# Delta-rule attention fused with a gelu MLP: orders, loads, PSUM banks and constant matmuls dealt anew

## The chip, the core and the metric

The kernel runs on one core of a Trainium2 chip. The metric is the device time of one execution in microseconds (us), the median of several runs. Five engines work side by side, each through its own queue of instructions in order: TensorE (PE, matmuls; its weight loads are shown as PEld), VectorE (DVE), ScalarE (ACT), GpSimd (POOL) and SyncE (SP, which here only issues DMA transfers). They wait for one another on semaphores. Matmul results land in PSUM, which has 8 banks of 512 f32 per partition; everything else lies in SBUF.

## The reference

Attention by the delta rule over 4 batches, 8 heads, 768 steps and head dimension 48, whose output is the input of a two-layer MLP with 3072 tokens, 384 to 2048 to 384:

```python
k_n = k / (np.linalg.norm(k, axis=-1, keepdims=True) + 1e-06)
state = np.zeros((B, H, D, D))
for t in range(S):
    y[:, :, t] = einsum('bhd,bhde->bhe', q[:, :, t], state)
    v_old = einsum('bhde,bhd->bhe', state, k_n[:, :, t])
    state = state + beta[:, :, t] * einsum('bhd,bhe->bhde', k_n[:, :, t], v[:, :, t] - v_old)
x = y.transpose(0, 2, 1, 3).reshape(B * S, H * D)
out = gelu_tanh(x @ w_in) @ w_out
```

Only q, k, v, beta and the two weights come in, in float32; out goes out in float32. Matmuls are in bfloat16.

## The kernel before

The sequence is cut into 12 chunks of 64 steps. Within a chunk the recurrence is a triangular system, which is inverted; between chunks a state S (48 x 48 for each of 32 heads) is carried. For each chunk c:

- `load` (L480) brings k (tiles kf), q (qf, two chunks at a time) and v (vf) over SP's queue, the first k in part over ACT's. `load_w1`, `load_w1x` and `load_w2` (L515 to L539) bring the MLP's weights over POOL's queue, after the first q.
- `prep` (L592) squares k (sq, on ACT or POOL), sums it on DVE (ss, L603), takes the root on ACT (sr) and the reciprocal on DVE (rn); from chunk 4 on the root is a short series of DVE operations (`norms`). ACT's function table is loaded once for the root and once for gelu; the root's first use is a small warm-up operation at the start.
- `prep2` (L658) scales k (Kn, on POOL or DVE) and transposes it on PE (L680); `prepq` (L636) does the same for q (L648). Copies out of PSUM (KQT) go to DVE or ACT.
- `own` (L722) multiplies the chunk's keys by themselves in small blocks of 32; DVE transposes the result (Tt). `solve8` (L768) inverts the small blocks of chunk 0 on DVE; `solve` (L752) does it on POOL for chunk 1, and then for units of two chunks (unit 1 is chunks 2 and 3). The results are scaled (XW), transposed back on DVE (`back`, L802, tiles TB), and from the unit on, one part is shifted between partitions by a DMA on SP's queue.
- `gram` (L693) makes the products of keys and queries with keys: G by ACT, DT by DVE with a mask.
- `inverse` (L893) builds the whole inverse from the blocks: WB, DI, ET and TT, with PE matmuls between.
- `state` (L1020) makes R = K S - V, U = T R, the new S, and the chunk's output x.
- `mlp` (L1210) takes tiles of one chunk (tiles 0 to 3) or two (tiles 4 to 7): groups of matmuls with gelu on ACT behind each (L260, gT), then the second layer in halves of 8 matmuls, an eviction to osb and a store on ACT's queue.

The order of the work is not found on the chip. Every call of `op` (L102) records one operation with a number, its functions for the engines that can do it, its tiles read and written, and its PSUM allocations. `schedule` (L136) then reads the string `ORDER` (L18): a letter for the engine (p PE, v DVE, a ACT, g POOL, s SP) and the number of the operation. Each engine does its operations in the order in which they stand there; `emit` (L167) adds the waits that the tiles and banks ask for. A word such as w12.5 is not an operation of the program: it puts 12 constant matmuls (`spin`, L411, 128 x 512 on a tile of zeros) on PSUM bank 5, whose result nobody reads. The string `BANK` (L78) has one digit for each PSUM allocation, its first bank. The loop at the file's end (L1272 on) only records.

The lines where operations run are often helpers: L251 is `f_tt` (two tensors), L256 `f_cp` (copy), L260 `f_act` (activation), L267 `f_mms` (all matmuls but transposes and constants), L275 `f_dma`.

Numbers that the texts below speak of: 47 and 48 load k of chunk 0, 49 and 50 load beta; 2 is the warm-up root on ACT, 82 Square, 86 root and 88 reciprocal (rn0) of chunk 0; 89 and 90 make K0; 153 Tt0, 265 Tt1; 156 to 173 are chunk 0's solve; 180 DT0_0, 186 DI0_0, 192 ET0_1, 198 to 204 TT0; 217 the last matmuls for x of chunk 0; 266 to 299 chunk 1's solve on POOL with XW0 (299); 72 to 81 the weights' loads; 130, 390 and 393 make K of chunks 3, 4 and 5; 400 and 603 are the masks bM0 and bM1; 135 is a cast of q; 307 and 308 WB of chunk 1, 313 its ET1_0, 316 the matmul group that reads it; 398 and 399 `own` of chunks 2 and 3; 401 to 433 unit 1's solve; 437 its `back`, 462 WB of chunk 3, 466 the first matmul group that reads that; 435 and 436 the shift of TB; 342 the last matmuls for x of chunk 1; 224 to 238 the first-layer groups of MLP tile 0; 1274 the last matmul group.

Of the kernel before, what the change touches and what calls it, by code (L numbers as in the profile page):

```python
# [30 lines left out]
p228 v381 g410 v382 a313 s151 g411 v329 p136 g412 p137 s150 a229 g413 v383 p316 v138 p318 g414 s149 a317 v384 g415  # L31
p438 a227 v385 s223 p230 g416 v386 v139 a439 g417 s222 p232 a231 v387 g418 s148 v388 p320 a233 g419 v389 p459 v319
g390 s220 p234 a460 v440 s221 p322 a235 v321 p456 v461 p324 g420 a323 s396 a457 g393 p326 p441 s397 v327 a519 p236
v325 v458 p333 a442 g421 v520 p238 g422 a334 p391 g423 a253 v443 g424 p330 g425 a239 v331 p338 g426 p394 a252 v332
g427 v335 p339 v392 p340 g428 p341 a578 s259 p342 g429 p240 g430 v344 s260 g431 a343 g433 v579 a395 s258 p254 a237
g432 v580 p601 s345 v437 p602 s261 a444 v434 p241 s346 v462 s347 v604 p255 s348 a242 p349 s436 v256 g605 p351 a350
s435 v581 p644 v582 a352 p466 s531 v583 g521 p353 v584 a645 v585 s532 v445 p245 g522 a354 v646 a257 g606 v586 v587
g607 p355 g608 v464 a467 g609 p336 v588 v446 p448 g610 v337 p246 g611 a449 g612 v589 g613 v463 p523 g614 v590 a356
v591 p474 g615 v592 a247 p450 g690 a447 p357 v451 p359 v475 g593 p524 a360 p452 v525 a358 p468 g616 v453 a526 s599
p361 g596 v469 s600 p454 a362 p363 s527 v455 g617 v691 p476 s530 g618 p470 a477 g619 p480 s529 p594 g620 a364 p481  # L40
s528 g621 p478 a482 g622 p365 v479 s483 g623 a771 g624 s489 v471 p366 g625 s491 a595 v772 g626 s488 g627 g628 p533
a243 v773 s490 p662 v774 g629 p597 a244 v775 s492 g630 v776 p370 g631 a598 v777 s487 v778 g632 v779 g633 v780 s703
a367 g634 p371 v781 g636 v782 a692 s702 v783 v784 v785 g635 p794 v534 a372 a663 p795 v640 g786 a465 p493 v647 p495
v664 a494 g693 p472 v797 a496 p497 s792 g883 p499 v473 a498 s793 v637 p535 v648 s638 g796 p501 a536 v884 s699 p539
a502 p540 p641 g798 s486 v541 p694 a642 s639 p503 a500 v643 s700 g799 p695 a504 g800 p505 v696 g801 s548 p507 a506
s546 v697 p537 a665 s547 p651 g789 p659 v652 p509 s701 a508 s550 v538 a660 g802 p790 s549 g803 a374 p510 v661 g804
s698 a958 g805 v791 s551 g806 a249 v649 p837 g807 p669 v959 s484 p653 a248 g808 s485 p514 g809 a838 v654 g810 a668
g811 v670 a511 p515 g812 g813 v667 v839 g814 p552 g815 v960 a516 v961 p655 g816 v962 a553 p834 g817 v656 p677 a835
g818 p554 v963 g819 a650 v678 p556 g820 a555 g821 p657 v836 a557 g822 p558 v658 a886 g823 v666 g824 p679 g825 a559
p683 p671 g826 a680 g827 p560 g828 v672 p681 a561 p562 v682 g829 p673 a563 v830 p684 p704 v674 s832 a685 p564 v705  # L50
s545 p675 a565 s831 p852 v676 a369 p566 v964 s542 a853 v965 p710 v966 s544 p706 v967 a567 p568 v968 s543 v969 a707
v970 v841 a368 v854 p711 p855 v971 a712 p569 v860 v972 v859 g973 a856 v833 s719 p787 a373 v842 s720 p573 v857 a858
g885 s717 s721 p974 v840 a517 s722 p708 v788 p862 a570 g976 p574 s718 v863 a512 s688 v709 s687 g981 p864 a575 p977
s689 a576 v865 p887 s686 g1133 p888 v975 p723 v889 p844 a724 p725 v845 a861 p727 a843 v978 a726 p979 v890 a728 p980
p846 v982 p729 p731 v847 g983 a730 p1019 a732 p866 p1022 g984 v867 p848 g985 a1023 g986 p733 v849 g987 p735 g988 v1024
g989 p1131 a736 g990 g991 p1132 a734 g992 a1020 p737 g993 v1021 p739 g994 a738 g995 v1134 p870 a740 g996 p741 g997
p743 v871 a742 g998 g999 p850 a518 g1000 p868 a744 g1001 p745 v869 g1002 v851 p747 g1003 a746 g1004 p872 a748 p876
g1005 p749 a873 g1006 g1007 p751 a750 g1008 p874 g1009 a752 p877 g1010 v875 p753 a878 g1011 g1012 p1037 g1013 p891
a754 p755 v892 a577 g1135 a513 v1015 p897 a571 p893 s1016 g1014 p756 v894 a1038 s716 s715 g1136 v1018 g1137 p898 p1040
s714 g1138 a899 p759 g1139 s1017 v757 g1140 a1041 g1141 v1039 s713 p760 g1142 a572 v1043 s907 g1143 a1025 v1042 g1144  # L60
s906 p763 g1145 v1044 s904 v1026 g1146 a758 s908 g1147 v1045 v761 p1171 g1148 s905 p1029 a1172 p764 g1149 s909 a1028
g1150 v1173 s903 g1151 v1030 p767 g1152 a765 s881 g1153 v1027 s879 g1154 p1047 s882 g1155 p895 p1031 g1156 s902 p910
g1157 v1032 s880 g1158 p768 a911 g1159 v1048 g1160 g1161 p912 v896 g1162 g1163 p1174 g1164 a913 p1049 g1165 p1033 a769
v1050 a1175 p914 g1166 v1034 p916 a915 p1055 v1170 a917 p1051 p918 v1052 p920 v1177 a919 v1056 p1035 a921 p1053 a762
v1036 p922 v1176 p924 a923 p1057 a925 p926 v1058 a1046 p928 a927 v1195 p1061 a929 v1167 p1059 p1062 v1060 s1169 p930
a1063 s900 p932 v1054 a931 s901 p1068 p1074 a933 v1069 p1189 s1168 p934 a1190 p936 v1191 a935 p1070 a937 p938 v1071
a770 p940 a939 v1197 p1181 a941 v1179 p1075 p1192 v1196 a1076 p942 v1182 a766 s1080 p943 a1180 s1078 s1067 p946 v944
s1064 a945 s1065 p947 a1193 s1066 v1194 s1077 p950 v1178 a948 s1081 a949 s1079 p951 s1082 p1199 a952 p1072 p1183 a953
p954 v1184 v1200 p1083 p955 v1073 a1084 p1207 a956 p1213 v1208 p1185 p1085 v1186 p1087 p1201 a1088 p1187 a1086 p1089
v1188 a957 v1202 p1091 a1090 p1209 a1198 p1203 v1210 a1092 p1093 v1204 p1095 a1094 p1214 a1096 p1205 a1215 p1211 p1097  # L70
v1212 p1099 a1098 v1206 p1216 a1100 p1101 v1217 p1103 a1102 p1218 a1104 p1105 v1219 p1107 a1106 p1220 a1108 p1109
p1111 a1110 p1221 a1112 p1113 v1222 p1115 a1114 s1226 p1116 s1227 s1225 s1224 p1119 a1117 s1228 s1223 p1120 p1123
a1121 p1124 p1229 a1125 p1231 a1230 p1233 a1118 p1235 a1232 p1237 p1239 p1241 a1240 p1127 a1242 a1236 p1243 a1234
a1238 p1245 a1244 p1247 a1246 p1249 p1251 a1250 p1253 a1122 p1255 a1126 p1257 a1252 a1248 p1259 p1261 a1260 a1254
p1128 a1256 a1258 p1262 v1129 a1130 p1265 a1263 a1264 p1266 p1269 p1270 p1273 v1271 v1267 a1268 p1274 a1272 a1275
a1276
"""
BANK = ("6031340340660141100441256766766777042000503073120036766677667154142444144220200367676676760000276766"  # L78
        "7676754202240042244430024042067667677676767676767024104052244440000220220666767676767676767661042024"
        "2242042530200022767767667676767676764000444440000044210001203141021031450102")  # L80


class Op:
# [1256 lines left out]
```

## Time and profile before

| | us |
|---|---|
| runs | 249.78, 252.54, 251.93 |
| median of the runs | 251.93 |
| span of the profiled execution | 249.4 |
| PE busy in it | 232.0 (93%) |
| DVE, ACT, POOL busy | 161.4, 139.0, 118.6 |
| matmul instructions | 5637 recorded, 87 of them constant |
| DMA moved | 23.84 MB, 96 GB/s |

The profile is of one execution, on one core; its span lies 0.4 us under the lowest of the three runs. In the profile's groups each line gives the code line, engine, operation, the tile written and read, the shape, then busy time and the mean of one. A line of the chain gives start, length, engine, tile and code line. "Issue" is time in which an engine waited for nothing that the profile shows. The granted clock of PE is given as a share of full speed. Idle time of an engine that is not the bottleneck costs nothing by itself.

### The profile page before, as it was taken

The page shows a single profiled execution, that of the slowest core. Times are in us where ns is not written, and L with a number is a line of the kernel's source. Part 1 is how long each engine was busy: PE and PEld are TensorE (multiplying, and loading weights), DVE is VectorE, ACT ScalarE, POOL GpSimd, SP SyncE. Part 2 cuts the span into 40 slices and gives each one's busy share as a digit, 9 for nine tenths or more (in the row PEclk, how much of TensorE's full clock was granted, in tenths as well). Part 3 has the DMA queues.
Part 4 walks back from the last instruction along what each step waited for, and adds up shares of the span by engine and source line. Part 5 has one row for each costly group of instructions (what it writes and reads, how often), then busy time and mean ns, then how long its engine had stood idle before and what let it go on. Part 6 is the DMA issues. An engine that isn't in the chain of part 4 may idle for free.

```text
span 249.4 us, 12386 instructions
## 1 busy us (share of the span) xinstructions
PE 232.0 (93%) x5637; PEld 155.0 (62%) x5637; DVE 161.4 (65%) x316; ACT 139.0 (56%) x262; POOL 118.6 (48%) x249
## 2 busy tenths in 40 slices
PE   7577896998999799999899999999999999999995
PEld 4334473587778658868766655666656665555562
DVE  6699989886799399896969653767772465100001
ACT  2744578587686466838564357535682247426600
POOL 3685796688389858588045589883000000000000
PEclk9999999799999799999999999999999999999999
DMA  6999969996740825550244000623135210000112
GB/s 157 209 196 168 159 116 211 159 214 107 184 87 19 192 52 112 122 137 7 57 111 91 5 20 23 149 57 63 37 76 134 78 37 3 8 11 32 66 63 96
DMA packets 64789, 23.84 MB, mean 96 GB/s; under 512 B 53600, under 2 KB 63840, under 8 KB 64736
## 3 DMA queue, kind: packets, MB, share of 16 engines
q1 hardware_dynamic: 58656, 14.89, 30.8%
q0 software_dynamic: 1056, 3.15, 7.3%
q10 hardware_dynamic: 5024, 5.02, 6.3%
q8 instruction: 44, 0.72, 1.2%
q14 instruction: 9, 0.07, 0.1%
HBM read 20.64 MB, written 4.72 MB: 102 GB/s over the span
## 4 chain that ended last, share of the span: by engine, by line
PE 81%; DVE 10%; DMA 2%; issue 2%; ACT 2%; POOL 0%; ACTq 0%; POOLq 0%
PE ps L267 76%; DMA kf<-in_k_dram 2%; PE ps L648 2%; PE ps L680 2%; PE ps L414 1%; DVE ss L603 1%; DVE WB L931 1%; ACT WB L915 1%; DVE TB L806 1%; DVE KQT L256 1%; DVE ps L846 1%; DVE Yf L251 1%; DVE Tt L837 1%; DVE btz L251 0%; DVE ps L786 0%
## 5 line engine op out<-in xcount | busy, mean ns | idle before, releaser
L260 ACT ACTIVATE gT<-ps 128x512 bf16<-128x512 f32 x96 | 55.9, 597 | 38.4 <-PE ps L267 36.8
L267 PE MATMUL ps<-x,W 128*128 128x256 bf16 (+1 forms) x384 | 72.2, 329 | 0.0
L267 PE MATMUL ps<-W,gT 128*128 128x384 bf16 x384 | 67.0, 328 | 0.0
L267 PEld LDWEIGHTS ps<-W,gT 128*128 128x128 bf16 x384 | 36.4, 98 | 23.9 <-issue 0.5
L267 PEld LDWEIGHTS ps<-x,W 128*128 128x128 bf16 x384 | 39.1, 115 | 16.3 <-issue 0.3
L762 POOL TENSOR_TENSOR Yf<-Yf,tmp 128x28 f32<-128x28 f32 (+13 forms) x84 | 28.8, 342 | 6.4
L759 POOL TENSOR_TENSOR tmp<-Yf 128x28 f32<-128x28 f32 (+13 forms) x84 | 28.1, 335 | 6.1
L251 DVE TENSOR_TENSOR TT<-ps,DI 128x768 bf16<-128x768 f32 (+2 forms) x30 | 20.2, 684 | 13.8 <-PE ps L267 13.5
L414 PE MATMUL ps<-wz 128*128 128x512 bf16 x87 | 23.3, 416 | 1.4 <-DVE wz L409 1.4
L251 POOL TENSOR_TENSOR Kn<-kf,rn 128x768 bf16<-128x768 f32 (+1 forms) x11 | 16.0, 1452 | 17.1 <-DVE rn L629 10.1
L267 PE MATMUL ps<-KQT 48*32 48x32 bf16 (+1 forms) x1152 | 18.7, 195 | 5.8 <-issue 2.7
L260 ACT ACTIVATE osb<-ps 128x384 f32<-128x384 f32 x18 | 8.8, 490 | 26.3 <-PE ps L267 26.3
L256 DVE COPY osb<-ps 128x384 f32<-128x384 f32 x6 | 3.2, 552 | 29.8 <-PE ps L267 29.8
L260 ACT ACTIVATE G<-ps 128x512 bf16<-128x512 f32 x24 | 14.3, 597 | 11.4 <-PE ps L267 7.7
L267 PEld LDWEIGHTS ps<-KQT 48*32 48x32 bf16 (+1 forms) x1152 | 13.6, 95 | 10.9 <-issue 5.0
L719 DVE TENSOR_TENSOR DT<-ps,mD 128x512 bf16<-128x512 f32 x24 | 16.3, 680 | 4.1 <-ACT G L260 4.1
L267 PE MATMUL ps<-TT,ET 64*64 64x32 bf16 (+1 forms) x768 | 16.4, 176 | 0.0
L267 PEld LDWEIGHTS ps<-TT,ET 64*64 64x64 bf16 x768 | 14.8, 109 | 2.2 <-DVE R L251 0.6
L414 PEld LDWEIGHTS ps<-wz 128*128 128x128 bf16 x87 | 8.7, 105 | 11.5 <-issue 3.0
L251 DVE TENSOR_TENSOR S<-ps,S 128x768 bf16<-128x768 f32 x10 | 9.5, 953 | 9.0 <-PE ps L267 8.9
L260 ACT ACTIVATE x<-ps 128x1024 bf16<-128x1024 f32 (+2 forms) x10 | 9.2, 916 | 8.1 <-PE ps L267 7.9
L251 DVE TENSOR_TENSOR R<-ps,vf 128x768 bf16<-128x768 f32 x11 | 10.4, 949 | 3.8 <-PE ps L267 3.8
(122 smaller groups left out, 333.2 us busy)
## 6 DMA issues: line engine op xcount, KB each, us to landing
qf<-in_q_dram SPq DMA_DIRECT2D x24, 192.0 KB, 4.4
kf<-in_k_dram SPq DMA_DIRECT2D x23, 192.0 KB, 4.9
vf<-in_v_dram SPq DMA_DIRECT2D x40, 96.0 KB, 3.2
out_dram<-osb ACTq DMA_DIRECT2D x16, 192.0 KB, 2.0
W<-in_moe_w_out_dram POOLq DMA_DIRECT2D x4, 384.0 KB, 6.7
out_dram<-osb ACTq DMA_DIRECT2D x16, 96.0 KB, 2.8
W<-in_moe_w_in_dram POOLq DMA_DIRECT2D x4, 192.0 KB, 8.7
vf<-in_v_dram SPq DMA_DIRECT2D x4, 192.0 KB, 11.3
```

The lines of the kernel that those rows point to most:

```text
L251: return lambda e: e.tensor_tensor(out() if callable(out) else out, a() if callable(a) else a, b() if callable(b) else b, op)
L256: return lambda e: e.tensor_copy(out, a() if callable(a) else a)
L260: return lambda e: e.activation(out, a() if callable(a) else a, func)
L267: ins = t.matmul(out, lhsT, rhs, start=st, stop=sp_, skip_group_check=skip)
L414: ins = e.matmul(psum[:, b, :], wz[:, 0:128], wz[:, :], start=True, stop=True)
L603: op({"dve": 0.95 * w}, {"dve": lambda e, u=u: e.tensor_reduce(ss[j][:, u], sq[:, u, :], AX.X, ALU.add)}, reads=[f"sq{n}"], writes=[f"ss{j ...
L648: ins = e.transpose(o[:, a, j], Qn[:, n, a, j, :, :].rearrange("q h d -> q (h d)"), identB[:, :])
L680: ins = e.transpose(tb()[:, m, :], t[:, 2 * m:2 * m + 2, :].rearrange("p h d -> p (h d)"), identB[:, :])
L719: op(d_ps(512), {"dve": lambda e: e.tensor_tensor(dv, gview(1)(), md, ALU.mult)}, reads=[h] + MD, writes=[dn])
L759: sop(nb * s * w, lambda e, s=s, w=w, tv=tv: e.tensor_tensor(tv, yf[:, :, s:s + 1, 0:s].to_broadcast([128, nb, w, s]), Yv()[:, :, s + 1:16 ...
L762: sop(nb * s * w, lambda e, s=s, tv=tv: e.tensor_tensor(Yv()[:, :, s + 1:16, 0:s], Yv()[:, :, s + 1:16, 0:s], tv, ALU.add), [YN, TN], [YN])
L806: op({"dve": 0.58}, {"dve": lambda e: e.transpose(dst, src)}, reads=reads, writes=writes)
```

## The change

Only the two strings are other. The operations are the same 1276, with the same shapes, tiles and dependences. The orders of all five engines are new, and with them the places of the loads and of the constant matmuls: 85 in 11 groups (1, 10, 6, 13, 9, 3, 29, 3, 7, 2, 2) in place of 87 in 11 groups (6, 12, 1, 1, 8, 4, 29, 1, 3, 12, 10). Some fifty operations, most of them copies out of PSUM, change between DVE and ACT, a few between POOL and another engine. The digits of the banks are new. SP has 138 operations and POOL 238 in both; DVE has 306 for 307, ACT 269 for 268. Code lines behind the strings are one lower. The core of the diff:

```diff
-v34 a50 g11 s49 v5 v0 g21 v46 a48 s47 g22 v6 g16 v8 v35 v41 g18 s54 v1 v4 a2 g13 g14 s55 g12 g19 v15 v45 s53 a26 v43
-v33 v10 s56 v3 w6.7 p61 v36 v37 v9 v38 s51 v42 v7 v40 s52 a82 g84 v63 s60 a24 g20 v85 g17 a29 v39 v62 a30 a31 v83 a32
-a23 v67 a86 s59 v70 a87 v64 v88 s57 a97 g75 v89 v65 g81 s58 w12.5 p91 v66 a98 p99 g90 v44 v92 g77 w1.4 p93 a103 v68
-p100 v94 g72 g76 a101 s96 p152 v104 g74 v153 g73 a105 w1.7 p181 a106 a182 v107 v154 g108 v156 v155 g69 w8.3 p109 v157
-v158 v159 a110 v160 v183 g80 s141 a102 v161 w4.5 p264 v162 v163 v164 p178 v265 a179 v165 g266 v166 a117 v167 v168 v169
-v170 a25 a28 g267 a27 v171 g268 g269 v172 g270 g271 v173 g272 g273 v174 g274 g275 v175 g276 g277 v176 a185 g278 g279
-s95 a184 v177 w29.3 p191 g280 p301 g281 v192 g282 a187 p189 v186 g283 v190 g284 a188 w1.5 p195 g285 v118 p193 g286
-a196 g287 a194 p199 v71 g288 v180 p197 g289 a200 g78 a119 p203 v198 a120 g290 a205 p201 v121 g291 v204 v122 g79 a202
-p209 a302 p206 g292 g293 s147 v207 a210 g294 g295 a125 v208 s140 v211 g296 w3.5 p215 v303 p216 g297 p217 s146 p304
-v218 a219 p212 p123 v126 a305 g299 v298 a127 a128 v129 a133 v306 g130 v300 s115 v124 a213 s113 g400 w12.7 p131 v308
-a309 s116 p398 v132 a311 s114 g603 v214 p399 a250 s111 p314 v401 a310 s112 a315 v251 s144 g402 s142 a375 v307 s143
-g403 g404 w10.6 p312 v376 a135 s145 g405 p224 g406 s262 g407 p226 v377 a225 g408 v378 s263 v379 p328 a134 g409 v380
...
-g427 v335 p339 v392 p340 g428 p341 a578 s259 p342 g429 p240 g430 v344 s260 g431 a343 g433 v579 a395 s258 p254 a237
...
-s435 v581 p644 v582 a352 p466 s531 v583 g521 p353 v584 a645 v585 s532 v445 p245 g522 a354 v646 a257 g606 v586 v587
...
-a1276
-BANK = ("6031340340660141100441256766766777042000503073120036766677667154142444144220200367676676760000276766"
...
+v0 g21 s47 a48 v45 g18 w1.3 g16 v34 v44 a50 v33 g13 s49 v46 w10.0 g14 g19 s55 v35 v10 s51 s52 a82 g84 w6.0 v83 g11 v85
+g12 s56 g22 p61 g17 a86 s54 a87 g20 v88 s53 v3 v36 v9 v5 v37 v15 v89 w13.0 s58 v1 v62 a2 v38 a32 v90 a103 v7 s95 a30
+v104 a25 p91 p93 s59 v63 a105 a26 v92 a94 v64 v67 v4 g81 v65 a97 v70 p152 v6 s60 v42 g77 v66 a106 a23 p99 a98 v107
+v153 g108 a24 p100 v154 w9.5 a101 g76 v155 s140 a102 v156 s141 p181 a27 p109 a182 v157 v158 v159 p178 a31 v68 a110
+w3.1 v160 g69 v161 v162 v163 a179 v164 v39 p264 v165 v166 v183 w29.7 v167 v168 v169 g117 v170 s57 v171 v180 g79 v8 s96
+v265 g74 g72 v172 g266 v173 v174 g267 v43 v175 g75 w3.4 v176 a184 g268 g73 v177 a185 p189 g269 p304 v187 a28 a186 p191
+g270 v190 g271 w7.2 v71 g272 v118 a29 a192 g273 g274 g275 a125 p301 g276 p193 g400 p195 a302 v194 a205 v40 v196 p197
+g277 v41 g78 v303 p199 a198 a305 g278 p201 v126 g80 a200 a202 p203 a119 g279 v306 a120 a188 g280 v121 a204 g281 a127
+a250 p209 g282 p206 g283 v210 w2.3 a207 g284 a128 g285 a211 v208 v251 g286 p215 p216 g287 p217 g288 v129 v122 g289
+g290 a218 g291 v219 s146 p123 g292 g293 s147 g294 p212 g295 v124 g130 p228 v213 p224 a229 g296 p131 a133 g297 p226
+v132 s113 p398 s115 a225 g299 v298 p399 s114 p234 v401 s116 a375 s111 a308 v300 g402 s112 v376 a307 p314 g403 a227
...
+g411 p322 g412 w2.7 s150 a139 v388 v323 p438 v389 a321 g390 p459 p326 a460 p324 a327 v461 a439 p232 g413 s396 a519
+v440 g414 p456 s397 p236 a325 g415 v520 a457 g393 p391 a252 v458 p330 p338 a237 v331 p339 g416 p333 v392 a332 g417
+p394 a334 g418 p238 a253 v395 g419 p254 a335 g420 a239 s259 p340 g421 p341 a578 s143 p441 p342 g422 a233 s261 g423
...
+g431 v581 p336 g432 v582 v583 p255 v604 p245 a256 g433 v434 p241 v584 g605 v437 s532 v585 a444 v462 s436 v257 g522
+p466 s435 v445 p246 g606 s531 v337 a467 g607 g608 s220 g609 a242 g610 p448 v247 p644 p474 g611 a645 v586 g521 p351
...
+a1250 p1269 p1247 p1273 a1248 a1126 p1266 p1270 a1267 a1268 p1262 v1271 a1272 p1274 a1263 a1264 a1275 a1276
+BANK = ("7301720430530101010120307666677776016301010106204426767677767151240000442230220477766667764220066767"
...
```

Loads of k stand ahead of those of beta on SP and ACT (s47, s49; a48, a50). ACT's Square (a82) stands ahead of the warm-up root (a2). Tt1 (v265) stands inside chunk 0's solve (156 to 173), and the weights' loads g75, g73, g78 and g80, the mask g400 and K3 (g130) stand inside chunk 1's solve (g266 to g299). In unit 1's solve (g402 to g433) now stand g603 and g135 beside g390 and g393. Four first-layer groups of MLP tile 0 (p228, p224, p226, p234) stand ahead of or among `own` of chunks 2 and 3 and chunk 1's inverse (p312, p314, p316), where 12 and 10 constant matmuls stood.

More of the change, by code (lines that the diff above doesn't have):

```diff
@@ L39 @@
[L39 to L43, printed above, removed]
@@ new lines @@
+a362 s600 p454 a526 g617 p357 v455 g618 v595 s530 p476 g619 p480 v691 a477 s529 g620 p363 g596 a358 p481 a364 p478
+s347 p365 a482 v479 g621 g622 a771 s489 g623 p597 g624 s488 a249 p470 v772 g625 a465 s491 p370 a598 g626 v471 s702
+g627 v773 g628 v774 s490 v775 g693 p533 v776 p662 p794 s492 v534 a663 g629 p371 s703 g630 v777 v664 s487 g631 g632
+p366 g633 v372 g634 g635 v778 a373 v779 a692 p641 p795 g636 v637 a243 p472 a642 s639 p497 v780 a367 v781 s346 v782
+p501 v783 a498 v784 v785 a883 v473 p493 g786 v643 a502 v797 p535 a494 p539 a536 s793 p499 v640 g798 s638 p495 a500
@@ new lines @@
+v884 s345 p659 p540 a496 s348 g799 p694 v541 a660 g1133 p503 p507 v661 a504 s551 g800 g801 p695 v648 s792 a508 p505
+v647 a665 s699 v649 v696 p537 g802 s549 p651 g803 p509 a697 v667 s548 v652 g804 s484 g805 a506 v538 g806 p837 s546
+p834 p510 g807 a838 s483 g808 a835 v839 g809 s486 a958 v836 g810 p677 s485 p653 a511 v959 g811 a650 p669 s550 g812
+p514 a248 v678 g813 s547 g814 v654 g815 p515 g789 v670 s542 p683 v666 s700 g816 p655 v516 g817 s698 p556 v656 g818
+p552 v960 g819 v961 g820 p671 a553 v962 p657 g821 a512 v963 g822 a557 p554 v658 g823 a668 v672 g824 p790 a555 g825
@@ new lines @@
+p562 v791 g826 a517 g827 g828 p679 a368 p558 v680 p673 g981 a559 p681 a563 v674 p684 p566 a374 g829 v682 a685 p560
+v830 p704 a561 v964 s832 p852 p675 v705 a513 s831 p564 a567 v676 s545 a853 v965 v833 p706 a565 s701 p568 v854 a858
+s543 v966 v841 v967 s544 v968 p855 p710 v969 a856 p573 a707 v857 a840 v970 v860 p708 v971 g886 v972 p711 v859 p862
+a369 p574 g973 v863 a885 v709 a712 p864 g976 a861 p787 v865 s719 a575 p974 s717 p887 a975 s718 p888 p569 s721 v889
+a788 s720 v890 p977 s722 a570 p844 s687 a571 p866 v845 s686 p979 p980 v842 s688 v867 p846 s689 v982 p725 p727 a726
@@ L83 @@
+a1250 p1269 p1247 p1273 a1248 a1126 p1266 p1270 a1267 a1268 p1262 v1271 a1272 p1274 a1263 a1264 a1275 a1276
+"""
+BANK = ("7301720430530101010120307666677776016301010106204426767677767151240000442230220477766667764220066767"
+        "7766712224222220432503304000266767767676767677667054420000244444022022224667676676777676676671522204"
+        "2204000302140422666776776767676767664042441400002243030204211170570353423165")
 class Op:
```

65 lines of the change are left out of this document (25 added, 40 removed).

## The prediction

> **What bounds the kernel now.** I read the page's busy shares and slices first, then the chain that ended last, then what TensorE (PE) waited for, then the clock by windows, then single rows around the places that these name.
>
> ```profile
> PE 232.0 (93%) x5637; PEld 155.0 (62%) x5637; DVE 161.4 (65%) x316; ACT 139.0 (56%) x262; POOL 118.6 (48%) x249
> ...
> PE   7577896998999799999899999999999999999995
> ...
> PEclk9999999799999799999999999999999999999999
> ...
> q8 instruction: 44, 0.72, 1.2%
> ```
>
> PE is busy for 232.0 of 249.4 us. Its lower digits are in the first eight slices (0 to 50 us); behind them it is nearly full, and no other engine is. The clock digit drops twice. Queue q8 brings instructions: 44 transfers, 0.72 MB in all, 16 KB each.
>
> ```profile
> 44.35 3.42 PE ps L414 x10
> 47.77 2.94 PE ps L267 x66
> ...
> 83.03 1.26 issue
> ...
> 123.03 0.75 issue
> ...
> 144.07 102.42 PE ps L267 x2080
> 246.51 0.49 ACT osb L260
> ```
>
> ```profile
> PE ps L267 <- issue: 4.7, 7, 1.3
> ```
>
> The chain of waits goes through DVE and ACT until 43 us, then stays on PE to the end: real matmuls (L267) are 76% of the span. The last constant matmuls (L414) end at 47.77. PE then loses time in pieces that wait for no engine ("issue": 4.7 us in 7 pieces, from the waits by engine). They lie at fixed places in PE's instruction stream: counted in instructions, each falls on 194 plus a multiple of 256, the size of one q8 transfer.
>
> ```profile
> 39.80:43.20 3.40, 1.31 (x89) 1.01 (x92) 3.37 (x6) 3.22 (x9) 2.46 (x3) 1.00 0.90 205
> 43.25:46.66 3.41, 3.41 (x86) 1.84 (x78) 3.11 (x6) 1.51 (x5) 1.27 (x1) 0.50 1.15 208
> 80.80:84.20 3.40, 2.23 (x117) 1.90 (x112) 1.64 (x3) 1.75 (x3) 2.85 (x8) 1.00 1.02 225
> 84.21:87.62 3.41, 3.33 (x89) 2.52 (x89) 0.95 (x2) 1.36 (x2) 2.79 (x9) 0.50 0.66 147
> ```
>
> The windows (first PE's busy time; behind the engines the granted clock, DMA share, GB/s) show two stretches of 3.41 us at half clock, each behind a stretch in which PE was busy for only 1.31 or 2.23 of 3.40 us. The first lies mostly over constant matmuls; the second lies over real work.
>
> **The change, part by part.** The base is the profiled execution, 249.4 us; the median shown, 251.93, lies 2.5 above it. I work out a difference on 249.4 and set it on the median.
>
> *Work on PE.* Both kernels hold the same real matmuls: 207.3 us, from each group's median row times its count. Constant matmuls are 85 for 87, at 0.216 us each 0.43 us less. That counts only where PE would not have waited anyhow; up to 48 us it waits, so 0.
>
> *Start, to the first state step.* Loads of k are now issued ahead of those of beta: 0.5 us earlier, from the 0.50 us issue row that stood before it on ACT. The Square of chunk 0 now precedes the first Sqrt, so ACT switches its function table once more in the critical part. The second load of before prices this:
>
> ```profile
> 37.78 0.21 ACT L611 ACTIVATE sr<-sr 128x16 f32<-128x16 f32 x1
> 38.02 1.28 ACT L260 ACT_TABLE_LOAD   x1
> 39.31 0.20 ACT L260 ACTIVATE warm<-warm 128x1 f32<-128x1 f32 x1
> ```
>
> 1.28 us, with 0.03 and 0.01 us to its neighbours. Before, the first load ran at 2.11 to 3.39, under the wait for k; now it lies between Square (to about 7.5) and Sqrt, which starts at 8.83. rn0 ends near 9.5 (before 10.35), because the constants' ACT copies moved behind it. DVE's memsets moved behind rn0 too (0.84 us), so K0 comes at 10.9, as before. Tt0 comes near 16.3 (before 15.02): DVE has more queued ahead. The solve on DVE wins about 1.3 back, if its two additions (1.59 and 1.48 us beside POOL's 1.84 and 1.43 us operations, against 0.59 for a transpose of twice the size) no longer run beside POOL. It starts at 18.7 (18.80).
> The Trainium skill, "ScalarE: Activation LUTs", "What ACT_TABLE_LOAD costs", gives every switch a drain of about 1.38 us besides 1.28 for the load. The rows above leave no room for a drain. By that rule K0 and all behind it would come an estimated 1.4 us later.
>
> *Chunk 1's solve on POOL and unit 1's behind it.* Tt1 moved inside DVE's solve, behind DT0_0: 24.75 (21.56), +3.2. Inside POOL's solve now lie two more W loads (0.6 each), bM0 (1.25) and K3 (1.48). POOL ends XW0 of chunk 1 near 44.1 to 44.6 (37.46). ACT carries DI0_0, ET0_1, a Square, G1_0 and R0 ahead of its TT0 copies, so x0's matmuls end near 40.1 (36.17). PE meanwhile does four groups of MLP tile 0 (0.65 each) from 41.8 on; they started at 48.07 before, behind 10 constants. The own products of chunks 2 and 3 end near 45.9 (43.80), and group 316 starts at 51.4 (51.54) after about 3 us of waiting for ET1_0, which stands behind DVE's norms; WB1 on ACT takes 2 x 0.9, where DVE took 2.58 for one beside POOL. At the last x1 matmuls (op 342; 63.56 before) PE has done 30.88 us of real work against 30.43 before, so parity is 64.0. I take 0 for the head; ends -3 (POOL's order taken as the clock) and +2.
>
> The next due date is unit 1's. The rows of before:
>
> ```profile
> 45.37 1.27 POOL L251 TENSOR_TENSOR Yf<-Tt,bM 128x512 f32<-128x512 f32 x1 [3.11 <-DVE Tt L875]
> ...
> 63.14 1.20 POOL L821 TENSOR_TENSOR XW<-Yf,nbT 128x256 bf16<-128x256 f32 x2
> ...
> 66.22 0.54 DVE L924 TENSOR_TENSOR WB<-TB,mB 128x768 bf16<-128x768 bf16 x1
> ...
> 70.32 0.42 PE L267 MATMUL ps<-WB,G 64*64 64x48 bf16 x32
> ```
>
> From the own products' end to POOL's start is 1.57 us, and the solve takes 64.34 - 45.37 = 18.97. Now bM1 (1.25) and one Q cast (0.89) stand inside it: 45.95 + 1.57 + 18.97 + 2.14 = 68.6. DVE's transpose (0.63), a norm (0.26) and WB (0.4) follow: 69.9. PE comes to op 466, which needs this WB, after the same work as before, thus at 70.3. Before, WB lay there 3.5 us early; now the cover is 0.4. All lateness in that chain beyond 0.4 us is PE idle, one for one, and all that PE saves before op 466 beyond 0.4 is lost there. SP's shift of TB for unit 1 now stands behind a load of k that waits for K5 and for older loads of q; its readers (DI of chunks 2 and 3, 0.35 each) are needed after op 466, and I count 0, with 1.7 (DVE's longest wait for that copy before) in the range. So the two fetch stalls at 57.24 and 66.03 (0.72, 0.33) count as 0.
>
> *Instruction transfers behind 70 us.* By the trace's records of q8 a transfer starts 0.4 to 2.3 us after its boundary and takes 0.88 to 1.75, so a stretch of 128 matmuls with little work outruns it. Before, the stretches under 3.3 us held 3.19, 3.20, 3.12, 2.89, 2.89 and 3.13 us of work, and three of them stalled: 1.26, 0.75, 0.62, sum 2.63 (0.44 per stretch). The new order has 2.81, 3.13 and 3.20, and one of 3.41 at the old 1.26. Four times 0.44 is 1.75: -0.9. Ends: -2.6 (none stalls) and +1.5 (each costs the mean of the three that did, 0.88, and one the largest).
>
> *Half clock behind 70 us.* The stretch 84.21 to 87.62 held 3.33 us of PE work at half rate, 1.67 lost. The stretch ahead of it held the 1.26 stall; with that gone PE is busy 3.4 of 3.4. I take -1.2 (ends -1.7 and 0), since PE can still wait there.
> The Trainium skill, "TensorE: Matmul & The Clock Gate", "What's actually happening", has the throttle return after at least one idle window. This trace halved the clock behind one with 2.23 of 3.40 us busy, so I go by the trace. By the page's words the new wait of about 3 us before 316 would be harmless; by the rows it can cost up to 1.7.
>
> *New waits among the full stretches.* Some fifty evictions and copies change between DVE and ACT, and banks are dealt anew. With before's durations the new order forces only four gaps of 0.07 us, but before's own cover there is thin (median 0.9 us). I take +0.7 (0 to +3).
>
> *The end.* The last matmul group and its eviction (0.49) and store stand last in both: 0.
>
> Sum: 0 - 0.9 - 1.2 + 0.7 = -1.4. On the profiled execution 248.0; on the median 250.5.
>
> **The rivals.**
> 1. *Unit 1's WB comes late (slower).* Place: op 466. For it: the cover of 0.4 us, a chain without slack from Tt1 on, POOL rows that stretch beside DVE (K1 1.84 against 1.48), and ACT and DVE queues that are 70 to 90% busy there. Against it: the head was planned as a whole, and POOL's wait for Tt1 may be shorter than I walked. The price is 1 us for each us that the own products end after 46.3. With 5 us late, 4.6, the time is 251.9 - 1.4 + 4.6 = 255.1; it is slower by 1% from 4.4 us on (an end near 50.4). The drain that the rows deny would be 1.4 of these.
> 2. *The head is shorter.* If Tt1 and the own products come 2 us before my walk, WB is early, the 1.05 us of fetch stalls before op 466 count, and idle time before 316 shrinks by 2 us: 250.5 - 2.0 - 0.7 = 247.8. For it: before waits 3.11 for Tt and 1.4 for a copy there; against it: x0 3.9 us later.
> 3. *The change does not do what it says.* Transfers stall as often as before (2.6) and the clock halves over real work again: +0.9 + 1.2 gives 252.6, no change. For it: stretches of 3.13 and 3.20 us both stalled and did not, before.
>
> **How the numbers follow.** Likeliest, the sum: 0.40, 250.5, itself 248.8 to 252.8. Late WB: 0.27, 255.1 (252.8 to 258). Shorter head: 0.23, 247.8 (246 to 249.5). No effect: 0.10, 252.6. A measurement here can tell about 1% from no change: 249.4 to 254.4. Faster: nearly all of the shorter head and a fifth of the likeliest, 0.30. Slower: most of the late WB and a little of the rest, 0.23. Same 0.47. The range for 8 in 10 is 247.0 to 256.0.
>
> **What would show it.** A table load between Square and Sqrt near 8 us with no gap beside it; Tt1 near 24.75 and own products ended near 46; MLP matmuls from about 42 us; PE's wait before op 466 under 0.5 us (over 3: rival 1); "issue" waits behind 70 us of about 1.8 in sum; clock 1.00 from 80 to 90 us; x1's last matmuls at 64 (61 to 62: rival 2). The forecast is wrong if the head's end moves by more than 2 us either way, or if a clock window halves over the full stretches.

## The result, and the profile after

| | before | changed |
|---|---|---|
| median, us | 252.24 | 262.62 |
| executions, us | 249.78, 252.54, 251.93, 254.93 | 261.52, 264.62, 260.53, 263.71 |
| profiled execution, span (its time) | 249.4 (249.78) | 259.8 (261.52) |
| PE busy, us | 232.0 | 235.8 |
| PE idle within the span, us | 17.4 | 24.0 |
| mean granted clock of PE | 0.986 | 0.947 |

The ratio is 1.0404 (95%: 1.0306 to 1.0502): slower by 4%. The forecast was 250.5, a little faster, with a range of 247 to 256: it was wrong in direction and size. Ratios here are over executions within 1.5% of a kernel's own fastest, so where a kernel spreads more, its ratio lies below that of the medians. The profiled execution of before is nearly its best: over 71 executions in all comparisons it averaged 253.8, and the changed kernel 261.2 over 14, so the typical loss is 7 to 8 us, while the two profiles differ by 10.4.

The page of the changed kernel:

```profile
PE 235.8 (91%) x5611; PEld 158.6 (61%) x5635; DVE 161.4 (62%) x311; ACT 136.9 (53%) x266; POOL 117.9 (45%) x249
...
PE   8779969768969996997999999999999998999995
...
PEclk9979975958998999799999999999999999999999
...
PE 61%; DVE 13%; ACT 10%; POOL 5%; issue 4%; DMA 3%; SPq 3%; POOLq 0%; ACTq 0%
```

The real work on PE is the same, and two constant matmuls fewer. Still PE is busy for 3.8 us more, and idle for 6.6 more. PE's digits of 7 or less now reach to slice 18 (about 120 us), where before, behind 50 us, only the slice at 81 to 87 had one, and the clock digit drops at five places, for two before. The chain holds 61% PE; it passes through POOL, DVE and SP as far as 123 us, and only from there lies mostly on PE (88%).

What PE waited for in the changed kernel (total, times, longest, in us):

```profile
PE ps L266 <- DVE ET L250: 3.3, 3, 2.9
PE ps L266 <- issue: 2.7, 10, 0.7
PE ps L266 <- DVE WB L923: 2.3, 1, 2.3
PE ps L266 <- DVE DT L718: 2.1, 1, 2.1
...
PE ps L266 <- DMA x<-x: 1.3, 1, 1.3
```

"Issue" ahead of real matmuls fell from 4.7 to 2.7, in the direction of the forecast. Behind 50 us four waits of over 1 us are new: for ET (group 316, at 54 us), WB (op 466, at 77), at 103 us and at 123 us. The third is put down to DT, which happened to end at 103.36. But by the kernel's own waits the group needs of DVE only a copy to osb that was done at 98.98, and of SP the copies of x of chunk 2, which landed at 103.27, just before the group began. So that wait and the last are the same thing: SP's copies of x for the MLP, two chunks in turn.

The windows of the changed kernel (PE's busy time first, granted clock third from the end):

```profile
73.69:77.10 3.41, 1.38 (x9) 0.60 (x7) 3.41 (x6) 0.55 (x2) 2.38 (x4) 1.00 0.36 70
77.11:80.51 3.40, 3.16 (x40) 1.55 (x40) 1.92 (x4) 2.33 (x6) 3.01 (x8) 0.50 0.62 125
100.99:104.40 3.41, 1.33 (x32) 1.27 (x27) 3.24 (x9) 0.41 (x2) 1.65 (x2) 1.00 0.30 68
104.42:107.82 3.40, 3.40 (x78) 2.30 (x76) 1.59 (x3) 2.97 (x5) 3.06 (x5) 0.50 0.53 102
```

Behind each of the two longer waits in full work, PE runs 3.4 us at half clock, in which it loses up to 1.7. There are eight such stretches in this execution (15.7 to 19.1, three at 36.1 to 46.4, two at 53.2 to 60.0, and these two) for two before.

The ends of operations in the two profiles give the ledger. At op 342 the changed kernel is 4.3 us behind at equal real work (it ends at 68.28 for 63.58, with 0.45 us more of the work done); behind op 466, 7.9; past before's own half-clock stretch at 84, 5.4; at 109 us 9; at 125 us 10.7; at the end 10.4.

### The profile page after: what moved, and what is told of

Its sections match the earlier page's. It is cut to its first block, busy times and chain, and to the rows that moved or that the text cites. A ratio compares the mean times of both kernels' runs of the same rounds, so it can differ in the third digit from the quotient of the medians.

```text
span 259.8 us, 12356 instructions
## 1 busy us (share of the span) xinstructions
PE 235.8 (91%) x5611; PEld 158.6 (61%) x5635; DVE 161.4 (62%) x311; ACT 136.9 (53%) x266; POOL 117.9 (45%) x249
## 4 chain that ended last, share of the span: by engine, by line
PE 61%; DVE 13%; ACT 10%; POOL 5%; issue 4%; DMA 3%; SPq 3%; POOLq 0%; ACTq 0%
PE ps L266 57%; SPq L274 3%; ACT gT L259 2%; DMA kf<-in_k_dram 2%; PE ps L413 2%; PE ps L679 2%; DVE DT L718 1%; DVE nw L250 1%; PE ps L647 1%; POOL Yf L761 1%; DMA x<-x 1%; POOL tmp L758 1%; POOL Kn L250 1%; ACT sq L259 1%; DVE TB L805 1%
## 5 line engine op out<-in xcount | busy, mean ns | idle before, releaser
L266 PE MATMUL ps<-x,W 128*128 128x256 bf16 (+1 forms) x366 | 71.4, 335 | 8.2 <-issue 2.1
L266 PE MATMUL ps<-W,gT 128*128 128x384 bf16 x384 | 68.1, 331 | 0.0
L761 POOL TENSOR_TENSOR Yf<-Yf,tmp 128x88 f32<-128x88 f32 (+13 forms) x84 | 30.4, 363 | 5.3
L255 DVE COPY osb<-ps 128x384 f32<-128x384 f32 x9 | 5.0, 555 | 37.5 <-PE ps L266 37.4
L413 PE MATMUL ps<-wz 128*128 128x512 bf16 x79 | 22.3, 434 | 2.5 <-DVE wz L408 1.3
L266 PE MATMUL ps<-KQT 48*32 48x32 bf16 (+1 forms) x1152 | 17.5, 194 | 2.5 <-DVE btd L568 2.0
L250 POOL TENSOR_TENSOR Kn<-kf,rn 128x768 bf16<-128x768 f32 x10 | 14.8, 1489 | 10.6 <-DVE rn L628 8.3
L259 ACT ACTIVATE osb<-ps 128x384 f32<-128x384 f32 x15 | 7.3, 490 | 15.1 <-PE ps L266 15.1
L602 DVE TENSOR_REDUCE ss<-sq 128x16 f32<-128x768 f32 (+1 forms) x13 | 11.4, 882 | 6.3 <-ACT sq L259 6.2
L914 ACT ACTIVATE WB<-TB,mBs 128x128 bf16<-128x128 bf16 (+1 forms) x24 | 8.9, 444 | 9.3 <-DVE TB L805 9.3
L250 DVE TENSOR_TENSOR R<-ps,vf 128x768 bf16<-128x768 f32 x11 | 10.5, 954 | 5.4 <-PE ps L266 5.4
```

The lines of the kernel that those rows point to most:

```text
L250: return lambda e: e.tensor_tensor(out() if callable(out) else out, a() if callable(a) else a, b() if callable(b) else b, op)
L255: return lambda e: e.tensor_copy(out, a() if callable(a) else a)
L259: return lambda e: e.activation(out, a() if callable(a) else a, func)
L266: ins = t.matmul(out, lhsT, rhs, start=st, stop=sp_, skip_group_check=skip)
L413: ins = e.matmul(psum[:, b, :], wz[:, 0:128], wz[:, :], start=True, stop=True)
L602: op({"dve": 0.95 * w}, {"dve": lambda e, u=u: e.tensor_reduce(ss[j][:, u], sq[:, u, :], AX.X, ALU.add)}, reads=[f"sq{n}"], writes=[f"ss{j ...
```

## Experiments

All ratios are to before on the same chip. The diffs show only the words around a move.

**Which part of the order holds the loss.** The order of one kernel up to op 342, the other's behind it, on all five queues:

```diff
-(order of after)
+(order of before up to p342) (rest of the order of after)
```

> A graft: the order (all engines) of the kernel before as far as the last x1 matmuls (op 342, 63.6 us there), then the order of the changed kernel for all that is left; banks likewise, with a few digits dealt anew where the two don't meet. At op 342 the changed kernel stood 4.5 us behind, at its end 10.4. Theory (the late head costs 4.5, and the wait before group 466 and the half clock behind it follow from the late POOL chain of the head): 3 to 5 us slower than before, some 6 less than the changed kernel, about 257. Rival (the order behind the head is as bad by itself): 5 to 7 us slower, about 259 to 260.

> The opposite graft: the changed kernel's order as far as op 342, then the order of before. Theory (the late head): 5 to 8 us slower than before, since op 466 must still wait for the late solve of unit 1. Rival (the head's 4.5 us are made good behind it, by slack in before's order, and the loss is in the new order behind): within 2 us of before.

g1_before_head: 255.99, 1.0061 (1.001 to 1.0112). g2_after_head (the reverse): 263.91, 1.0342 (1.0215 to 1.0469). Most of the loss lies in the order ahead of op 342; the new order behind it costs 0.6%, if anything. One thing of the ledger stays, though, with before's order ahead. In g1's profile (259.94 us, the slowest of its ten executions) PE still waits for the copies of x, 2.79 us at 97.3 and 2.05 at 117.1:

```profile
PE ps L266 <- DMA x<-x: 4.8, 2, 2.8
```

So these two waits belong to the order behind 342. Against them, before's stall at 83 and the half clock behind it are gone there. For g2_after_head the seam adds a wait of its own; its rows of DVE, then PE:

```profile
81.80 0.44 DVE L924 TENSOR_TENSOR DI<-TB,mB 128x384 bf16<-128x384 bf16 x1 [5.61 <-DMA TB<-TB]
...
83.63 0.69 PE L648 MATMUL ps<-identB,Qn 128*128 128x128 bf16 x8 [4.87 <-DVE S L251]
```

DVE waits 5.61 us for SP's shift of TB, PE 4.87 behind it. So 3.4% is not the head's cost alone.

**Cuts within the head**, at Tt1 and at x of chunk 0, same form of edit (c_a: the changed order first; c_b: before's first).

> Graft: the changed kernel's order of all engines as far as Tt1 of chunk 1 (DVE op 265, about 24.7 us), then the order of before. Since the loss sits in the order ahead of op 342 (3.4% with that part alone), this tells whether the start makes it: table load, loads of k first, memsets behind rn0, Tt1 3.1 us late, POOL's wait for k of chunk 2. Theory (the start makes the lateness, which later stages only carry): 2 to 4% slower than before. Rival (the start's 3 us are made good; the loss is made between 25 and 68 us): within 1%.

> Graft: the changed kernel's order as far as the last matmuls for x of chunk 0 (op 217, 40.8 us there, 36.2 before), then the order of before. Theory (start): as slow as the graft that ends at Tt1, 2 to 4%. Rival (the ACT and POOL queues between 25 and 41 us: TT0 behind other copies, loads, bM0 and K3 inside the solve of chunk 1): clearly slower than the graft at Tt1, near the 3.4% of the graft at op 342. Third (the part from 41 to 68 us, with MLP groups ahead of own): both grafts within 1%.

> The opposite: the order of before as far as Tt1 of chunk 1 (21.6 us there), then the changed kernel's order for the rest. Theory (start): within 1% of before, as with before's order to op 342 (0.6%). Rivals (the loss is made later): 2.5 to 4% slower.

> The order of before as far as op 217, then the changed kernel's. Theory (start) and the second (25 to 41 us): within 1% of before. Third (41 to 68 us): 2 to 4% slower.

266.0 (1.0485), 262.41 (1.0231), 267.52 (1.0526), 264.63 (1.0397). All four are slower by 2 to 5% in the middle of their intervals. The last two wait 6.92 and 6.33 us right at the seam. The first two do not, but PE loses over 10 us to "issue" (10.1 and 10.5 on real matmuls). The grafts also do not keep the number of constant matmuls: 126, 105, 46 and 67, for 87 and 85, since the two orders have them on different sides of the cut. So these runs do not say which part of the head is to blame.

**Constant matmuls ahead of the waits**, to keep PE busy:

```diff
-v70 p152
+v70 w8.1 p152
-v383 p316
+v383 w12.5 p316
-g522 p466
+g522 w9.2 p466
-s639 p497
+s639 w8.1 p497
-s698 p556
+s698 w5.7 p556
```

> The changed kernel with 42 more constant matmuls (9.1 us at full clock), put only where PE waits: 8 before own of chunk 0, 12 before group 316, 9 before group 466, 8 and 5 before the MLP groups that wait for the copies of x of chunks 2 and 3. No wait of real work is taken away. Theory (each wait is followed by a stretch of 3.41 us at half clock, and that is a large part of the loss): half clock falls from eight stretches to three (36 to 46 us stay), 53 to 60, 77 to 80 and 104 to 108 go, and the time falls by 4 to 6 us to about 257. Rival (only the waits themselves cost, the half clock lies under them): no change within 1 us, 261 to 263.

267.88, 1.0527 (1.0447 to 1.0607): worse. The waits at 316 and 466 went to 0.38 and 0, and half clock to five stretches, but what PE waited for now reads

```profile
PE ps L267 <- issue: 10.5, 9, 2.3
```

The 42 constants shift where the boundaries of the instruction transfers fall among the real matmuls, and single stalls of 2.03, 1.57, 2.26 and 1.26 us appear behind 70 us. What half clock alone costs cannot be judged by this run.

**SP's copies of x without loads between them:**

```diff
-p597 s488 g624
+p597 g624
...
-s489 g623
+s489 s488 s491 s490 s492 s487 g623
...
-s551 g800
+s551 s549 s548 s546 s550 s547 g800
```

> The changed kernel with the six small copies of x of chunk 2, and those of chunk 3, put one behind the other on SP's queue, ahead of the loads that stood between them. Theory (loads between the copies make the MLP groups of tiles 2 and 3 wait 2.08 and 1.31 us, and the first of these brings a half-clock stretch): both waits go below 0.3 us, the stretch at 104 us goes, the time falls by 3.5 to 5 us to about 258. Rival (the copies are late because x is late, or the loads then come late and something else waits): the time falls by less than 1.5 us.

262.93, 1.0341 (1.0268 to 1.0414). The copies land at 98.38 and 112.03 (103.27 and 122.82), and both waits for them are gone. So is the half-clock stretch at 104. But PE now waits 2.21 us at 115.8 for R of chunk 4 on DVE. R's own inputs were there at 112.4; ahead of it in DVE's queue stands the sum for chunk 11, which waits for ACT's Square, and that for a load of k. The rows of ACT and DVE:

```profile
115.29 0.84 ACT L259 ACTIVATE sq<-kf 128x768 f32<-128x768 f32 x1 [3.79 <-DMA kf<-in_k_dram]
...
116.17 0.95 DVE L602 TENSOR_REDUCE ss<-sq 128x16 f32<-128x768 f32 x1 [3.83 <-ACT sq L259]
```

The load landed at 115.27, as in the changed kernel (115.35): it is no later, but what needs PE now comes earlier and meets it. Windows of this run:

```profile
104.80:108.20 3.40, 3.40 (x97) 3.16 (x87) 3.21 (x6) 2.62 (x7) 2.93 (x8) 1.00 0.39 69
...
115.00:118.40 3.40, 1.19 (x38) 0.63 (x35) 2.23 (x3) 1.62 (x3) 2.77 (x9) 1.00 0.55 118
118.40:121.80 3.40, 2.98 (x54) 2.31 (x43) 3.37 (x7) 0.00 (x0) 3.26 (x6) 0.51 0.58 148
121.80:125.20 3.40, 3.40 (x73) 2.66 (x72) 1.64 (x5) 1.52 (x3) 0.48 (x1) 0.50 0.13 31
```

The half clock moved with the wait: here it follows the wait and is not at a fixed place of the work. It lasted three windows (118.4 to 128.7), though PE was busy for most of them, so that one wait of 2.21 was followed by 10.2 us at half clock.

**DVE's order at 316 and 466:** both halves of ET1 (315, 313) ahead of the sum and norms; unit 2's transposition Tt (604), with its product on POOL (605), behind WB. The second kernel also puts the state's S copy (214) earlier (the last two lines).

```diff
-v376 a307
+a307
...
-p312 v377
+p312 v315 v313 v376 v377
...
-v462 s436
+v462 v604 g605 s436
...
-v213 p224
+v213 v214 p224
```

> The changed kernel with two moves on DVE: ET1 of chunk 1 ahead of the sum and norms of chunks 4 and 5, and unit 2's transposition Tt (with its product on POOL) behind TB and WB of chunk 3. Theory (DVE's queue makes both waits; the half clock behind them follows): PE's wait before group 316 falls from 2.85 to about 1 us, that before 466 from 2.28 to under 0.3, at least two of the half-clock stretches at 53 to 60 and 77 to 80 go, time 5 to 7 us less, about 256. Rival (the late start of POOL's solve of unit 1 sets the wait before 466, whatever DVE does first): 466 still waits over 1.5 us and the time falls by less than 3 us.

> The changed kernel with three DVE moves in the head: S3 of chunk 0 straight behind S (43.5 instead of 55.2 us), ET1 of chunk 1 ahead of the norms, and unit 2's Tt behind TB and WB of chunk 3. Without the first, ET1 came earlier and the next PE group waited 2.83 us for S3 in its place. Theory (DVE's order from 41 to 77 us): PE's wait before 316 and the one for S3 both go below 1.2, 466 waits under 1, time falls by 3 to 5 us. Rival (POOL's chain): under 1.5 us.

e3_dve: 262.51, 1.0253 (1.0153 to 1.0353). 316 no longer waits, but the next group does, 2.83 us for S; 466 waits 0.87. f2_dve2: 259.99, 1.0232 (1.0145 to 1.0318): both are gone, 466 waits 0.28, but PE waits 2.64 at 81.4 for an operation of DVE that the profile gives as DT, and 2.0 at 120 for x. It has the lowest median of the repairs, with an interval that overlaps the others', and is still 2.3% slower than before.

**POOL's queue in the head.** e6_pool: the weights' loads into POOL's idle time at 13 to 20 us, the Square of chunk 2 (117) to ACT. f1_pool2: 117 to ACT, two loads earlier. f3_both: that and f2_dve2.

```diff
-v169 g117 v170
+v169 v170
...
-v176 a184
+v176 a117 a184
```

> The changed kernel with POOL's queue freed ahead of and inside the solve of chunk 1: the seven W loads go to places where POOL waited (13 to 20 us), and the square of chunk 2, for which POOL waited 2.92 us on a load of k, goes back to ACT. Masks and K3 stay inside the solve. Theory (POOL's queue makes the own products and unit 1's solve late): the product with Tt1 starts at 24.7 instead of 26.6, XW0 of chunk 1 ends at 42 to 43 instead of 46.1, the wait before 466 goes below 0.5, and the time falls by 3 to 5 us, to about 258. Rival (DVE and ACT set the head, POOL is only beside it): the solve ends earlier, the own products not, and the time stays within 1.5 us of 262.

> The changed kernel with one POOL part undone in the head: the square of chunk 2 goes back from POOL (where it waited 2.92 us for its load and stood ahead of the product with Tt1) to ACT, and two W loads move from inside chunk 1's solve to just ahead of it. Loads move by no more than 5 us, so that transfers should not meet as in the run where they moved by 10. Theory (the POOL chain from Tt1 on is what is late): the product starts at 24.7 instead of 26.6, XW0 of chunk 1 ends near 43 instead of 46.1, and the time falls by 2 to 3 us, 1 per cent. Rival (DVE's queue is what is late; the POOL chain would only wait for it): XW0 earlier, unit 1's WB not, time within 1 us of the changed kernel.

> Both parts together, POOL and DVE. If both are causes in one chain, the gains add: 5 to 7 us less than the changed kernel, 256, about 1.5% slower than before. If only one counts, as that one alone.

e6_pool: 268.12, 1.0468 (1.0318 to 1.0618). k of chunk 3 (kf) now lands at 40.1, and ACT, which has its Square queued ahead of chunk 0's TT copies, waits; its row:

```profile
40.21 0.84 ACT L259 ACTIVATE sq<-kf 128x768 f32<-128x768 f32 x1 [8.18 <-DMA kf<-in_k_dram]
```

f1_pool2: 262.68, 1.0343. Tt1's product ends at 26.0 (27.89 in the changed kernel), yet XW0 ends at 46.33, as without the edit (46.06). The gain went into a wait: K3 stands inside POOL's solve, and in this execution k of chunk 3 landed at 34.4 (28.4 in the changed kernel), so its norms came late:

```profile
41.76 2.06 POOL L250 TENSOR_TENSOR Kn<-kf,rn 128x768 bf16<-128x768 f32 x1 [2.23 <-DVE rn L612]
```

So this run does not clear POOL's queue. f3_both: 263.26, 1.0287. The two repairs do not add.

**Chunk 3's k.** The changed kernel once more, with a profile:

```diff
 (no edit)
```

> The changed kernel itself again, on the chip of the next three, as their base: 3 to 5% slower than before by every theory.

261.34 over ten executions, 254.72 to 267.8 (1.0148, 1.0078 to 1.0218; by the medians 1.032). In this profile the same load landed at 36.5 (28.4 in the first), and the row and wait are

```profile
36.57 0.84 ACT L259 ACTIVATE sq<-kf 128x768 f32<-128x768 f32 x1 [5.76 <-DMA kf<-in_k_dram]
```

```profile
PE ps L266 <- ACT TT L259: 6.8, 3, 6.0
```

So one load that varies by 8 us stops PE for 6 us in one execution and not in another. k1_sq3 puts chunk 3's Square and norms behind those copies; k2_sq3_dve adds f2_dve2's edits.

```diff
-g275 a125 p301
+g275 p301
...
-a211 v208 v251
+a211 a125 v208 v126
-a218 g291 v219
+a218 a127 a128 g291 v219 v129
```

> The changed kernel with one ACT part of the head undone: the square of chunk 3, which waits for its load of k, stands behind the copies of TT0 and U of chunk 0 again (as in the kernel before), with its sum, root and the square of chunk 4 moved along. In five runs of this head that load landed at 34.4 to 40.1 us, and TT0 came 2.3 to 2.5 us behind it each time; in the others it landed at 27 to 32.5 and TT0 came at 33 to 35. Theory (the copy that PE waits for stands behind an operation that waits for a load, and the load's landing varies by 10 us): TT0 at 34 or earlier whenever the load lands, the median 2 to 4 us below that of the changed kernel (about 258 to 259), the slowest run below 264, half-clock stretches fewer by one. Rival (the late load is a chance of some runs; the rest of the head is late without it): median within 1 us of 261.5.

> The same with the three DVE moves of f2_dve2 (S3, ET1, and TB ahead of unit 2's Tt). Theory (late load on ACT first, DVE's order from 41 to 77 us second): 4 to 6 us below the changed kernel, about 256, 1 to 2% slower than before. Rival (waits only change places): no better than the first alone.

k1_sq3: 261.96 (260.25 to 262.96 over six), 1.0317 (1.0268 to 1.0366). k2_sq3_dve: 261.58, 1.0275 (1.0216 to 1.0334). In k2_sq3_dve k landed at 35.6 and the first copy of TT0 was still done at 34.0: the exposure is gone. The spread of k1_sq3 is 2.7 us over six executions, for 13 over ten, and the median is the same. So that load does not make the loss; that it makes part of the spread is likely by these few.

**Before, altered.** e4_before_w4 keeps PE busy through the stall at 83; e7_before_move12 moves 12 constants from before p131 to before p91.

```diff
-v691 p476
+v691 w4.5 p476
```

```diff
-w12.5 p91
+w12.5 w12.0 p91
-g400 w12.7 p131
+g400 p131
```

> The kernel before with 4 constant matmuls (0.86 us of work) more, ahead of R of chunk 2, in the stretch of instructions that held 3.19 us of work and stalled 1.26 us at 83.0. Theory (the stretch outruns the transfer of instructions, and the stall brings the half clock at 84.2): the stall goes below 0.4 us, the clock stays full from 80 to 90, and the kernel gains 1 to 2.5 us, although it does more. Rival (the stall has its size from the place in the stream and moves along; or the clock falls because the matmuls there are small): same or 0.9 us slower.

> The kernel before with its 12 constant matmuls of 37 to 40 us moved to 8.2 us, where PE waited 2.8 us anyhow; the number of instructions ahead of everything behind 40 us is unchanged. PE then waits from 37 to 39.8. Theory (a wait brings a stretch at half clock, and that costs): one or two more half-clock stretches between 38 and 47, and 1 to 3 us slower. Rival (half clock around there lies under waits for DVE): within 0.7 us.

e4_before_w4: 254.19, 1.0057 (1.0005 to 1.0109): the stall at 83 and the half clock behind it are gone, other stalls stand at 59 (1.13) and 68 (0.60), and nothing is gained. e7_before_move12: 253.83, 1.001 (0.9961 to 1.0059), with four half-clock stretches from 34.3 to 48.0. In the head, where PE waits for other engines anyhow, they cost nothing that this run can measure.

**What the half clock follows.** In all 20 profiles, from 70 us to 235, PE has 41 gaps over 1.2 us. Of 21 gaps of 2.0 us or more, 17 have half clock behind them, for one to three windows of 3.4 us; of the 20 shorter ones, 8. Only two stretches follow none of them. Over the 14 executions of the changed kernel, windows at half clock, worked out from the mean granted clock, go from 3 to 10 and the time with them, 1.6 us for each (correlation 0.87). This is not yet a price, since a wait lengthens the time by itself and brings a window too.

No version was faster than before. The repairs of 316 and 466 (f2_dve2) and of the copies of x (e2_xfirst) were not run together.

## Why the prediction was wrong

The sum in the prediction's own terms, between the two profiled executions:

| step | forecast | measured |
|---|---|---|
| head, to op 342 | 0 (-3 to +2) | +4.3 |
| WB at op 466 (rival 1) | 0 beyond a cover of 0.4 | +2.3 |
| instruction transfers behind 70 us | -0.9 | -1.8 (2.63 to 0.86, one piece over 0.2, at 214.5) |
| half clock behind 70 us | -1.2 | +1.7 (two stretches for one, up to 1.7 each) |
| new waits | +0.7 (0 to +3) | +3.4 (x copies, 2.08 and 1.31) |
| sum | -1.4 | 9.9 of 10.4 |

*"I take 0 for the head."* This is the first step that failed. Its start came out: rn0 at 9.46 (9.5), Tt0 16.12 (16.3), Tt1 24.67 (24.75). That is in part luck. The table load between Square and root costs what its row said, and nothing is lost around it. But ACT in the changed kernel reads

```profile
5.57 1.28 ACT L259 ACT_TABLE_LOAD   x1 [5.57 <-DMA kf<-in_k_dram]
6.87 0.52 ACT L259 ACTIVATE sq<-kf 128x384 f32<-128x384 f32 x1
7.41 1.28 ACT L259 ACT_TABLE_LOAD   x1
8.70 0.22 ACT L259 ACTIVATE sr<-ss 128x16 f32<-128x16 f32 x1
```

Another load of 1.28 us stands ahead of Square, and it began only when k had landed. Before, that load ran under the wait for k, and the sum has no second one. It was made good by k itself, which landed at 5.50 for 7.03 before: 1.5 us earlier, where 0.5 was forecast.

From there the walk left the loads of k out. POOL's Square of chunk 2 waited 2.92 us for k, which landed at 23.4 (13.3 before), and Tt1's product ended at 27.89; Tt1 at 24.75 and the 1.29 us of the product would give 26.0. XW0 ended at 46.06 (44.1 to 44.6), own at 48.10 (45.9). PE's wait of 3 us before 316 came as forecast in size (2.85), but the group began at 53.9, not 51.4. Op 342 ended at 68.28 for 64.0, 4.3 late; the 1.8 beyond that 2.5 are most likely of the two half-clock stretches behind the wait (53.2 to 60.0), which the prediction had priced at up to 1.7 and not taken. f1 took the late Square of chunk 2 away and k1 the load ahead of TT0, and neither brought the time down; but in f1 a late load took the gain, and the two were not run together. Which queue of the head is the first stays open.

The size is of one pair of executions. The same order as far as op 342 ended there at 65.31 in the profile of g2, at 65.99 in that of e2 and at 71.70 in that of f0; before's order ended there at 66.12 in g1.

The Trainium skill, "TensorE: Matmul & The Clock Gate", "What's actually happening", lets the throttle return after at least one idle window. In the windows above it returned behind windows in which PE was busy for 1.38 and 1.33 of 3.41 us, and the prediction's rows of before show the same; the measurement decides.

*Rival 1 happened, and its size was wrong.* The cover was 0.4, as worked out. WB came at 77.30 for 69.9, PE at 75.07 for 70.3: 7.4 less 4.8 less 0.4 is 2.2, and the wait was 2.28. But of the 7.4 only 2.2 came from own. Of the rest, 2.6 arose in POOL's solve (23.7 us for 21.1) and 2.9 in DVE behind it, less 0.2 for an earlier start; POOL, then DVE:

```profile
60.08 1.48 POOL L250 TENSOR_TENSOR Kn<-kf,rn 128x768 bf16<-128x768 f32 x1 [3.51 <-DVE rn L628]
```

```profile
73.33 1.24 DVE L874 STREAM_TRANSPOSE Tt<-ps 128x1024 f32<-128x1024 f32 x1
74.49 0.60 DVE L805 STREAM_TRANSPOSE TB<-XW 128x256 f32<-128x256 f32 x1
74.94 1.02 DVE L250 TENSOR_TENSOR nw<-sr,ss 128x32 f32<-128x32 f32 x1
75.89 0.63 DVE L805 STREAM_TRANSPOSE TB<-XW 128x256 f32<-128x256 f32 x1
76.37 0.36 DVE L624 SCALAR_TENSOR_TENSOR nw<-nw,sr 128x32 f32<-128x32 f32 x1
76.66 0.64 DVE L923 TENSOR_TENSOR WB<-TB,mB 128x768 bf16<-128x768 bf16 x1
```

K of chunk 4 stands inside unit 1's solve in both kernels, but now it waits 3.51 us for DVE's norms (0.50 before), and DVE takes 4.2 us from XW to WB (73.15 to 77.30), where the prediction counted 1.3: unit 2's transpose and two norms stand between. This wait is the firmest part of the ledger: it came in each profile of the changed order that left DVE's queue there alone, with 1.66 (e2), 2.25 (f0), 2.29 (e6), 2.18 (f1) and 2.22 us (k1).

*"New waits", 0 to +3.* Mis-sized, for a reason: SP's copies of x were not followed. x of chunk 2 was itself 5.7 us late (the first copy was issued at 93.04, before at 87.31), and with loads of k between them the six copies took 10.2 us, to 103.27, for 6.0 before, to 93.28.

*Half clock, -1.2.* The stretch at 84 did go, but the waits at 77 and 103 brought their own. It was counted as an entry of its own, when it is a surcharge on most waits of 2 us or more. Both signs that the prediction names for its own failure came: the end of the head moved by over 2 us, and windows halved over full stretches.

*Rival 3* (the change does nothing) and *rival 2* fail with the sum. Right were the price of a table load, the cover of 0.4 us at op 466, and the direction of the instruction stalls.

Shown by the runs: most of the loss lies in the order ahead of 342 and what it hands on, while the waits for x are of the order behind it; each of the four waits can be taken away; the time then hardly moves, and the profiles show another wait in its place. Only argued: the split of the ledger, which is of two single executions, and which operation of the head is late first.

## What to carry to other kernels

Where a plan brings an engine to a due date with a few tenths of a us to spare, price the lateness of every queue that feeds it, SP's included, one for one up to the next due date, and add the half-clock stretch that most waits of 2 us brought here. Do not put an operation that waits for a load ahead of one that the bound engine needs: it showed at TT0 in f0, at K3 in f1 and at R in e2. Take the base from several executions: one profiled execution of this kernel lay 4 us under its mean.

## What the runs showed of the hardware

- Of PE gaps of 2.0 us or more in full work, 17 of 21 were followed by 3.4 to 10.2 us at half clock; in e2 it moved with the wait.
- In the head half clock also came behind a stretch in which PE was busy for 97% of the time (39.6 to 43.0 of the changed kernel, already at half clock, about half of it with matmuls of 64 rows and columns), and did not come in before behind 9.1 to 12.5, busy for 45% with full-size ones. What the gate counts was not settled.
- A norm of DVE on 32 elements took 1.14 us at 51.59 and 1.02 at 74.94, for 0.18 to 0.21 at 50.88, 55.18 and 56.99; the two long ones each ended within 0.1 us of an operation of POOL (52.67, 75.91). The Trainium skill, "SBUF — State Buffer", "Who interferes with whom", has an operation of VectorE with two SBUF inputs wait for one of GpSimd that reads SBUF; these rows agree.
- With 42 more constants on PE, "issue" went from 2.7 to 10.5 us. But a stall also varies by itself: in eleven profiles with the same PE order as far as op 234 (at about 50 us), the one in that group took 0.36 (f3) to 2.52 us (e6).
- A load of 192 KB landed anywhere between 27 and 36.5 us in executions of nearly the same order.
